# A fused attention and expert kernel on one core: the scatter of an expert's rows is moved behind its test, the gathers into the front half of the tile

## The chip, the cores and the metric

The kernel runs on one core of a Trainium2 chip, as one program. The metric is the device time in microseconds of one execution; the median of the runs shown is 710.27 us.

## The reference, cut to what matters

Attention and a first dense layer make `x`, 1536 rows of 512. The change lies in the last layer, a mixture of eight experts: a row that is not skipped goes through the one expert that its gate picks, and every other row is copied.

```python
def _moe2_ref(x, w_skip, w_gate, w1, w2):
    do_compute = x @ w_skip > 0
    out = x.copy()
    xc = x[do_compute]
    logits = xc @ w_gate
    e_idx = np.argmax(logits, axis=1)
    ...
    for e in range(E):
        mask = e_idx == e
        h = np.maximum(xc[mask] @ w1[e], 0.0)
        y[mask] = gate_w[mask, None] * (h @ w2[e])
    out[do_compute] = xc + y
    return out
```

Per expert `w1` is 512 x 1024 and `w2` 1024 x 512, both float32.

## The kernel before

The first stages (attention, then the first dense layer) fill the time up to about 480 us and are not touched. The second dense layer writes `x` twice, to the scratch tensor `x2d` and to the output, and the routing writes a list `LT`: for each expert up to twelve blocks of 128 rows, each with a row to fetch, a row to write and the gate's weight. Unused places name a row out of bounds, which the scatter leaves out.

`moe2` then goes through the experts. Each expert has one **tile** of 128 rows that always runs, and up to eleven **further tiles** (`extras`), nested in branches on the number of rows that the routing counted, a value that only the run knows. In this run expert 0 has five further tiles, expert 7 has one, the six between have none.

All matmuls are done on values split in two: a high part that ScalarE writes (`w2h`, `xh`, `th`) and the rest that is left, which VectorE or GpSimd subtracts (`w2l`, `xl`, `tl`). A tile is: 12 matmuls for the first half of the hidden layer and the relu, 12 for the second half with the transposes of the first half in between (`hidden`), 24 matmuls into `y`, and `finish`, where VectorE scales `y`, adds it to the fetched rows and leaves the result in the same buffer. In the middle of the second part `prepare(e + 1)` transposes and splits the rows of the next expert.

The order on each engine is the order in which the code is written; nothing reorders it. Four things run beside the matmuls of tile e:

- **Weights.** The sixteen half chunks of expert e + 1 are split (`Moe2Weights.split`, lines 371 to 379), dealt out over the tile by `aside`. ScalarE writes each high part; the rest is VectorE's for twelve of them and GpSimd's for numbers 3, 7, 11 and 15 (`POOLK`). Raw weights arrive in a ring of nine buffers of 512 KB; after each odd half chunk its buffer is free and `load` issues the next load from SyncE's queue, in order, so a load behind one that waits also waits. High and low parts have two sets, used by experts in turn, so expert e + 1's set is free to be written only when expert e - 1 and its further tiles are done.
- **Gathers.** `gather(e + 2)` fetches the rows of the expert after next with an indirect DMA from GpSimd's queue, into one of three buffers `XF`. It takes the buffer that expert e - 1 used, so it needs that expert's scatter to have landed.
- **The pull.** `enlist(e)` and `pull(0)` on GpSimd copy the list of the expert's further blocks and fetch the first of them into `XE`, before it is known whether a further tile runs.
- **Scatter.** At the end of `finish` an indirect DMA on GpSimd's queue writes the tile's rows to the output. The two scatters of an expert with a further tile both write the output and are kept in order.

The test for a further tile (line 619) is taken by each engine for itself. On its untaken side an engine adds to its semaphores what the branch would have added. GpSimd also does so for the semaphores of its DMAs (`INC_SWDGE_SEM` in the trace), and it first waits until the DMAs before the branch have landed. `hint` tells TensorE's queue early which way the branch goes.

Of the kernel before, what the change touches and what calls it, by code (L numbers as in the profile page):

```python
# [22 lines left out]
NT = B * S  # L23
DM = H * D
F1 = 768
E2 = 8
# [485 lines left out]
def fetch(nc, xg, x2d, m):  # L512
    nc.gpsimd.indirect_dma_start(out=xg, out_offset=None, in_=x2d,  # L513
                                 in_offset=bass.IndirectOffsetOnAxis(ap=m[:, 0:1], axis=0))


def moe2(tc, nc, m2, ident, rt, XF, x2d, out):
    pool = tc.alloc_tile_pool(name="m2", bufs=1, side="left", reuse_waits="tile")
    LT, extra = rt["LT"], rt["plan"]
    XH = [[pool.tile([P, NC1, P], F32R, name=f"x{x}{i}") for x in "hl"] for i in range(3)]  # L520
    m2.open(pool, RING[1])
    XE = [pool.tile([P, DM], F32, name=f"xe{i}") for i in range(3)]
    PL = [pool.tile([P, CMAX, 4], I32, name=f"pl{i}") for i in range(2)]
    PM = [pool.tile([P, 4], I32, name=f"pm{i}") for i in range(3)]
    nc.gpsimd.memset(PL[0], 0)
    with tc.tile_pool(name="ps3", bufs=1, space=PSUM, reuse_waits="tile") as ps:

        tiles = [{"e": e, "xg": XF[e % 3], "m": LT[:, e * CMAX], "x": XH[e % 2]} for e in range(E2)]

        def gather(e):  # L530
            if e < E2:
                fetch(nc, tiles[e]["xg"], x2d, tiles[e]["m"])

        def enlist(e):
            nc.gpsimd.tensor_copy(out=PL[0][:, 0:CMAX - 1], in_=LT[:, e * CMAX + 1:(e + 1) * CMAX])  # L535

        def pull(i):
            nc.gpsimd.tensor_copy(out=PM[i % 3], in_=PL[0][:, 0])  # L538
            fetch(nc, XE[i % 3], x2d, PM[i % 3])
            nc.gpsimd.tensor_copy(out=PL[1], in_=PL[0])  # L540
            nc.gpsimd.tensor_copy(out=PL[0][:, 0:CMAX - 1], in_=PL[1][:, 1:CMAX])  # L541

        def turn(src):
            tp = ps.tile([P, 4, P], F32, tag="tp", name="tp", bufs=3)
            for c in range(4):
                nc.tensor.transpose(tp[:, c], src[:, c * P:(c + 1) * P], ident)
            return tp

        def halves(src, h, l):
            nc.scalar.activation(out=h, in_=src, func=AF.Copy)  # L550
            nc.vector.tensor_tensor(out=l, in0=src, in1=h.bitcast(F32), op=ALU.subtract)  # L551

        def prepare(e):
            if e < E2:
                halves(turn(tiles[e]["xg"]), *tiles[e]["x"])

        def ready(i):
            halves(turn(XE[i]), *XH[2])

        def hidden(d, n):  # L560
            d["hT", n] = h, l = [pool.tile([P, 4, P], F32R, tag="t" + x, name="t" + x, bufs=2) for x in "hl"]
            halves(turn(d["r", n]), h, l)

        def mm1(d, n, cr):
            if ("h", n) not in d:
                d["h", n] = ps.tile([P, 512], F32, tag="h", name="h", bufs=3)
            h, l = d["x"]
            for c in cr:
                for i, (a, lo) in enumerate(((h, 0), (h, 1), (l, 0))):
                    nc.tensor.matmul(d["h", n], lhsT=a[:, c], rhs=m2.w1(d["e"], c, n, lo),  # L570
                                     start=(c == 0 and i == 0), stop=(c == NC1 - 1 and i == 2))

        def relu(d, n):
            d["r", n] = pool.tile([P, 512], F32, tag="r", name="r", bufs=2)
            nc.scalar.activation(out=d["r", n], in_=d["h", n], func=AF.Relu)

        def mm2(d, fr):
            if fr[0] == 0:
                d["y"] = ps.tile([P, DM], F32, tag="y", name="y", bufs=2)
            for f in fr:  # L580
                h, l = d["hT", f // 4]
                for i, (a, lo) in enumerate(((h, 0), (h, 1), (l, 0))):
                    nc.tensor.matmul(d["y"], lhsT=a[:, f % 4], rhs=m2.w2(d["e"], f, lo),  # L583
                                     start=(f == 0 and i == 0), stop=(f == NF2 - 1 and i == 2))

        def finish(d):
            ot = d["xg"]
            nc.vector.scalar_tensor_tensor(out=ot, in0=d["y"], scalar=d["m"][:, 2:3].bitcast(F32),
                                           in1=ot, op0=ALU.mult, op1=ALU.add)
            nc.gpsimd.indirect_dma_start(  # L590
                out=out, out_offset=bass.IndirectOffsetOnAxis(ap=d["m"][:, 1:2], axis=0),
                in_=ot, in_offset=None, bounds_check=NT - 1, oob_is_err=False)

        def tile(d, aside=lambda n: None, ahead=lambda: None, then=lambda: None):
            aside(0)
            mm1(d, 0, (0, 1, 2, 3))
            relu(d, 0)
            aside(1)
            mm1(d, 1, (0, 1))
            hidden(d, 0)  # L600
            mm1(d, 1, (2, 3))
            relu(d, 1)
            ahead()
            aside(2)
            mm2(d, (0, 1))
            hidden(d, 1)
            aside(3)
            mm2(d, (2, 3))
            then()
            aside(4)  # L610
            mm2(d, (4, 5, 6, 7))
            finish(d)

        def hint(e, i):
            tc.mark_branch_hint_location(f"x{e}_{i}", extra[e] > i, engines=[mybir.EngineType.PE])

        def extras(d, i=0):
            last = i + 1 == CMAX - 1
            with tc.If(extra[d["e"]] > i, label=f"x{d['e']}_{i}"):  # L619
                def more():  # L620
                    return tc.If(extra[d["e"]] > i + 1)

                def then():
                    with more():
                        ready((i + 1) % 3)

                if i == 0:
                    ready(0)
                if not last:
                    with more():  # L630
                        pull(i + 1)
                tile({"e": d["e"], "xg": XE[i % 3], "m": PM[i % 3], "x": XH[2]},
                     ahead=lambda: last or hint(d["e"], i + 1), then=(lambda: None) if last else then)
                if not last:
                    extras(d, i + 1)

        prepare(0)
        gather(1)
        for e in range(E2):
            todo = list(range(16)) if e + 1 < E2 else []  # L640

            def aside(n):
                k = DEAL[e > 0][n]
                for j in todo[:k]:
                    m2.split(e + 1, j)
                    m2.load(1)
                del todo[:k]

            m2.load(sum(RING) if e == 0 else 0)

            def ahead():
                enlist(e)
                pull(0)
                hint(e, 0)

            def then():
                prepare(e + 1)
                gather(e + 2)

            tile(tiles[e], aside, ahead, then)  # L660
            extras(tiles[e])
    pool.release()


# [455 lines left out]
```

## Time and profile before

| what | us |
|---|---|
| median of the runs shown (3) | 710.27 (709.78 to 713.14) |
| the profiled execution | 706.31 |
| its span, first to last instruction | 704.4 |
| TensorE busy in the span | 649.9 (92%) |
| VectorE busy | 421.7 (60%) |
| ScalarE busy | 336.3 (48%) |
| GpSimd busy | 311.4 (44%) |
| DMA, mean rate | 124 GB/s |

The profiled execution takes 1.9 us more than its span and lies 0.56% below the median. Shares of busy time are means over stages with different limits, so they say little on the last stage, which is the last third of the span; there windows by tile are read. A row of the view by time has start, duration, engine, line, operation, output and inputs, and in brackets how long the engine was idle before it and what ended that. A name such as `POOLq L619` is an instruction of the engine's queue itself (a branch, a wait), which counts as idle time of the engine.

### The profile page before, as it was taken

The page shows a single profiled execution, that of the slowest core. Times are in us where ns is not written, and L with a number is a line of the kernel's source. Part 1 is how long each engine was busy: PE and PEld are TensorE (multiplying, and loading weights), DVE is VectorE, ACT ScalarE, POOL GpSimd, SP SyncE. Part 2 cuts the span into 40 slices and gives each one's busy share as a digit, 9 for nine tenths or more (in the row PEclk, how much of TensorE's full clock was granted, in tenths as well). Part 3 has the DMA queues.
Part 4 walks back from the last instruction along what each step waited for, and adds up shares of the span by engine and source line. Part 5 has one row for each costly group of instructions (what it writes and reads, how often), then busy time and mean ns, then how long its engine had stood idle before and what let it go on. Part 6 is the DMA issues. An engine that isn't in the chain of part 4 may idle for free. (4 is left out here: it accounts for less than half of the span.)

```text
span 704.4 us, 9584 instructions
## 1 busy us (share of the span) xinstructions
PE 649.9 (92%) x3361; PEld 476.7 (68%) x3361; DVE 421.7 (60%) x652; ACT 336.3 (48%) x648; POOL 311.4 (44%) x246
## 2 busy tenths in 40 slices
PE   6798999999999998999999999999799988897884
PEld 2444555555555546999999997886588766675663
DVE  4698868878685483656656652753522276676511
ACT  6665666766665661323223222554322266676510
POOL 1495767767676861322122200343413065555620
PEclk9799999999999999999999999999999999999997
DMA  7454214213003003024304131679701057777510
GB/s 254 168 157 157 90 45 157 69 46 112 23 1 116 0 1 151 19 102 150 117 32 150 44 137 60 209 265 309 275 31 54 23 182 253 257 245 270 182 35 12
DMA packets 31472, 87.40 MB, mean 124 GB/s; under 512 B 4066, under 2 KB 4450, under 8 KB 30608
## 3 DMA queue, kind: packets, MB, share of 16 engines
q1 hardware_dynamic: 28144, 78.21, 32.0%
q0 software_dynamic: 3232, 8.07, 3.6%
q8 instruction: 40, 0.66, 0.4%
q14 instruction: 56, 0.46, 0.2%
HBM read 77.35 MB, written 10.18 MB: 124 GB/s over the span
## 5 line engine op out<-in xcount | busy, mean ns | idle before, releaser
L832 POOL TENSOR_TENSOR sum<-sum,Pt 128x768 f32<-128x768 f32 x60 | 117.1, 1955 | 32.0 <-ACT Pt L827 31.9
L827 ACT ACTIVATE Pt<-psb 128x384 f32<-128x384 f32 x192 | 83.7, 488 | 63.0 <-PE psb L825 62.2
L792 DVE TENSOR_REDUCE negm<-psa 128x1 f32<-128x768 f32 x86 | 82.0, 954 | 42.7 <-PE psa L790 42.4
L217 PE MATMUL m<-xh,whi 128*128 128x384 f32 x288 | 97.7, 339 | 2.9 <-DVEq L923 2.8
L217 PE MATMUL m<-xl,whi 128*128 128x384 f32 x288 | 96.6, 335 | 0.0
L217 PE MATMUL m<-xh,wlo 128*128 128x384 f32 x288 | 96.6, 335 | 0.0
L377 DVE TENSOR_TENSOR w2l<-ring,w2h 128x512 fp32r<-128x512 f32 x100 | 75.7, 808 | 33.3 <-ACT w2h L375 21.5
L839 PE MATMUL pso<-Pt,V 128*64 128x384 f32 x384 | 82.5, 511 | 0.0
L375 ACT ACTIVATE w2h<-ring 128x512 fp32r<-128x512 f32 x128 | 71.7, 623 | 20.9 <-PEq L619 11.3
L823 PE MATMUL psb<-S 128*128 128x384 f32 x192 | 75.8, 395 | 0.3 <-ACT S L767 0.3
L823 PEld LDWEIGHTS psb<-S 128*128 128x128 f32 x192 | 36.4, 190 | 53.3 <-ACT Pt L827 23.1
L825 PE MATMUL psb<-S 128*128 128x384 f32 x192 | 65.4, 340 | 0.0
L217 PEld LDWEIGHTS m<-xh,whi 128*128 128x128 f32 x288 | 54.1, 188 | 6.0 <-DVEq L923 3.5
L377 POOL TENSOR_TENSOR w2l<-ring,w2h 128x512 fp32r<-128x512 f32 x28 | 38.8, 1393 | 40.6 <-DMA ring<-in_dram 20.5
L217 PEld LDWEIGHTS m<-xh,wlo 128*128 128x128 f32 x288 | 54.1, 188 | 0.0
L217 PEld LDWEIGHTS m<-xl,whi 128*128 128x128 f32 x288 | 54.1, 188 | 0.0
L334 POOL TENSOR_TENSOR wlo<-wide,whi 128x512 fp32r<-128x512 f32 x18 | 23.4, 1300 | 69.4 <-ACT whi L333 53.7
L570 PE MATMUL h<-w2h,xh 128*128 128x512 f32 x112 | 48.1, 429 | 6.0 <-ACTq L619 2.7
L551 DVE TENSOR_TENSOR tl<-tp,th 128x512 fp32r<-128x512 f32 x28 | 19.3, 689 | 55.8 <-ACT th L550 50.3
L583 PE MATMUL y<-w2h,th 128*128 128x512 f32 x112 | 48.1, 430 | 3.3 <-ACT th L550 2.8
L583 PE MATMUL y<-w2h,tl 128*128 128x512 f32 x112 | 45.6, 407 | 4.4 <-DVE tl L551 4.3
L570 PE MATMUL h<-w2h,xl 128*128 128x512 f32 x112 | 46.1, 412 | 1.9 <-DVE xl L551 1.9
(185 smaller groups left out, 1219.4 us busy)
## 6 DMA issues: line engine op xcount, KB each, us to landing
ring<-in_dram SPq DMA_DIRECT2D x64, 512.0 KB
R<-in_dram SPq DMA_DIRECT2D x32, 384.0 KB
wraw<-in_dram SPq DMA_DIRECT2D x6, 1536.0 KB
Z<-in_dram SPq DMA_DIRECT2D x16, 384.0 KB
V<-in_dram SPq DMA_DIRECT2D x8, 384.0 KB
oraw<-in_dram SPq DMA_DIRECT2D x6, 512.0 KB
traw<-in_dram SPq DMA_DIRECT2D x6, 512.0 KB
x2d<-x SPq DMA_DIRECT2D x12, 256.0 KB
```

What stands on the lines that cost most here:

```text
L217: nc.tensor.matmul(pt, lhsT=l[:, w, c], rhs=r[b][c][:, a:a + BLK], start=(n == 0), stop=(n == 3 * NC1 - 1))
L334: self.nc.gpsimd.tensor_tensor(out=lo, in0=self.x, in1=hi.bitcast(F32), op=ALU.subtract)
L375: self.nc.scalar.activation(out=h, in_=r, func=AF.Copy)
L377: eng.tensor_tensor(out=l, in0=r, in1=h.bitcast(F32), op=ALU.subtract)
L570: nc.tensor.matmul(d["h", n], lhsT=a[:, c], rhs=m2.w1(d["e"], c, n, lo), start=(c == 0 and i == 0), stop=(c == NC1 - 1 and i == 2))
L583: nc.tensor.matmul(d["y"], lhsT=a[:, f % 4], rhs=m2.w2(d["e"], f, lo), start=(f == 0 and i == 0), stop=(f == NF2 - 1 and i == 2))
L792: nc.vector.tensor_reduce(out=d["negm"][:, t, h:h + 1], in_=tl[:, 0:S], axis=AX.X, op=ALU.max, negate=True)
L823: nc.tensor.matmul(tl, lhsT=S1[:, 2 + h, k * P:(k + 1) * P], rhs=S1[:, h, cut(j)], start=True, stop=False, skip_group_check=True)
L825: nc.tensor.matmul(tl, lhsT=S2[:, 2 + h, k * P:(k + 1) * P], rhs=S2[:, h, cut(j)], start=False, stop=True, skip_group_check=True)
L827: nc.scalar.activation(out=pt[:, cut(j)], in_=tl, func=AF.Exp, scale=0.125)
L832: eng.tensor_tensor(out=d["sum", h], in0=d["P", h, 0] if k == 1 else d["sum", h], in1=pt, op=ALU.add)
L839: nc.tensor.matmul(d["o"][64 * h:64 * h + 64, i], lhsT=d["V"][:, k, h], rhs=d["P", h, k][:, i * BLK:(i + 1) * BLK], start=(k == 0), stop=( ...
```

## The change

The scatter is taken out of `finish` and becomes a function of its own. For the tile of expert e it is called after the expert's test and its further tiles: at the head of the round of expert e + 1, and for the last expert at the program's end. A further tile's scatter stays where it was. Enlist and pull move from the middle of the tile to its head, behind that scatter; for expert 0 ahead of the whole loop. The gather for expert e + 2 moves from the last third of the tile to a point behind the first group of matmuls (`mid`).

```diff
@@ finish, tile
             nc.vector.scalar_tensor_tensor(out=ot, in0=d["y"], scalar=d["m"][:, 2:3].bitcast(F32),
                                            in1=ot, op0=ALU.mult, op1=ALU.add)
+
+        def scatter(d):
             nc.gpsimd.indirect_dma_start(
                 out=out, out_offset=bass.IndirectOffsetOnAxis(ap=d["m"][:, 1:2], axis=0),
-                in_=ot, in_offset=None, bounds_check=NT - 1, oob_is_err=False)
-
-        def tile(d, aside=lambda n: None, ahead=lambda: None, then=lambda: None):
+                in_=d["xg"], in_offset=None, bounds_check=NT - 1, oob_is_err=False)
+
+        def tile(d, aside=lambda n: None, mid=lambda: None, ahead=lambda: None, then=lambda: None):
             aside(0)
             mm1(d, 0, (0, 1, 2, 3))
             relu(d, 0)
             aside(1)
+            mid()
             mm1(d, 1, (0, 1))
@@ extras
-                tile({"e": d["e"], "xg": XE[i % 3], "m": PM[i % 3], "x": XH[2]},
-                     ahead=lambda: last or hint(d["e"], i + 1), then=(lambda: None) if last else then)
+                x = {"e": d["e"], "xg": XE[i % 3], "m": PM[i % 3], "x": XH[2]}
+                tile(x, ahead=lambda: last or hint(d["e"], i + 1), then=(lambda: None) if last else then)
+                scatter(x)
@@ the loop over experts
         prepare(0)
+        enlist(0)
+        pull(0)
         gather(1)
         for e in range(E2):
...
-            def ahead():
+            if e:
+                scatter(tiles[e - 1])
                 enlist(e)
                 pull(0)
-                hint(e, 0)
-
-            def then():
-                prepare(e + 1)
-                gather(e + 2)
-
-            tile(tiles[e], aside, ahead, then)
+            tile(tiles[e], aside, lambda: gather(e + 2), lambda: hint(e, 0), lambda: prepare(e + 1))
             extras(tiles[e])
+        scatter(tiles[E2 - 1])
```

GpSimd is the one engine on which rows change places. Its order for the round of expert 1 before, from behind expert 0's further tiles to the test (`w2l` are splits, `pl` and `pm` the list and its first block, `xe` the pulled rows, `xf` the gathered ones):

```order
L377 TENSOR_TENSOR w2l01_4194<-ring03_4183,w2h01_4186 128x512
L377 TENSOR_TENSOR w2l03_4196<-ring00_4180,w2h03_4188 128x512
L535 COPY pl0_4812<-LT_4459 128x44
L538 COPY pm0_4814<-pl0_4812 128x4
L513 DMA xe0_4809<-x2d_74,pm0_4814 128x512
L540 COPY pl1_4813<-pl0_4812 128x48
L541 COPY pl0_4812<-pl1_4813 128x44
L377 TENSOR_TENSOR w2l05_4198<-ring02_4182,w2h05_4190 128x512
L513 DMA xf0_4201<-x2d_74,LT_4459 128x512
L377 TENSOR_TENSOR w2l07_4200<-ring11_4790,w2h07_4192 128x512
L590 DMA out_0_dram<-xf1_4202,LT_4459 1536x512
L619 COMPARE_AND_BRANCH
```

The same round after the change:

```order
L592 DMA out_0_dram<-xf0_4201,LT_4459 1536x512
L535 COPY pl0_4812<-LT_4459 128x44
L538 COPY pm0_4814<-pl0_4812 128x4
L513 DMA xe0_4809<-x2d_74,pm0_4814 128x512
L540 COPY pl1_4813<-pl0_4812 128x48
L541 COPY pl0_4812<-pl1_4813 128x44
L377 TENSOR_TENSOR w2l01_4194<-ring03_4183,w2h01_4186 128x512
L377 TENSOR_TENSOR w2l03_4196<-ring00_4180,w2h03_4188 128x512
L513 DMA xf0_4201<-x2d_74,LT_4459 128x512
L377 TENSOR_TENSOR w2l05_4198<-ring02_4182,w2h05_4190 128x512
L377 TENSOR_TENSOR w2l07_4200<-ring11_4790,w2h07_4192 128x512
L622 COMPARE_AND_BRANCH
```

The scatter ahead of the test was that of this expert (`xf1`); now the round begins with that of the expert before (`xf0`), and the gather that refills `xf0` follows in the same round. The last DMA ahead of the test is now this gather.

The last round, that of expert 7, before:

```order
L535 COPY pl0_4812<-LT_4459 128x44
L538 COPY pm0_4814<-pl0_4812 128x4
L513 DMA xe0_4809<-x2d_74,pm0_4814 128x512
L540 COPY pl1_4813<-pl0_4812 128x48
L541 COPY pl0_4812<-pl1_4813 128x44
L590 DMA out_0_dram<-xf1_4202,LT_4459 1536x512
L619 COMPARE_AND_BRANCH
```

And the end of GpSimd's program after the change, behind the nested further tiles of expert 7 (an `ISA` row is the untaken side of a test, with its waits; 1118 is the end of the program):

```order
L622 ISA
L622 UNCONDITIONAL_BRANCH
L592 DMA out_0_dram<-xf1_4202,LT_4459 1536x512
L1118 UNCONDITIONAL_BRANCH
L1118 ISA
```

Expert 7's own scatter (`xf1`), once ahead of the test for its further tiles, is now the program's last work.

## Rows read from the trace of the kernel before

**Rows 1.** Windows by tile, tiles 1 to 6: stretch, us, busy by engine, clock, DMA.
```profile
566.05:582.93 16.88, 13.21 (x61) 9.95 (x61) 12.08 (x17) 10.88 (x21) 12.18 (x12) 1.00 0.64 219
582.93:598.02 15.09, 14.91 (x60) 11.05 (x61) 10.30 (x16) 11.11 (x22) 8.00 (x9) 0.89 0.69 242
598.02:614.81 16.79, 14.78 (x61) 11.09 (x61) 11.28 (x17) 11.31 (x22) 8.97 (x11) 0.90 0.75 257
614.81:628.40 13.59, 13.29 (x60) 9.88 (x61) 11.97 (x17) 11.09 (x22) 5.30 (x6) 1.00 0.83 275
628.40:647.68 19.28, 14.76 (x61) 11.02 (x61) 11.79 (x17) 11.76 (x22) 11.78 (x13) 0.91 0.74 251
647.68:664.38 16.70, 13.43 (x61) 9.88 (x61) 12.33 (x17) 11.52 (x21) 10.19 (x11) 1.00 0.70 239
```

**Rows 2.** SyncE's waits, tiles 1 to 6: us in total, times, longest.
```profile
SPq L365 <- POOL w2l L377: 38.9, 9, 9.1
SPq L368 <- POOL w2l L377: 18.3, 8, 3.8
```

**Rows 3.** GpSimd by time, one round: start, us, instruction, idle before it.
```profile
628.33 2.54 POOL L377 TENSOR_TENSOR w2l<-ring,w2h 128x512 fp32r<-128x512 f32 x2 [7.96 <-PE y L583]
630.83 0.21 POOL L535 COPY pl<-LT 128x44 int32<-128x44 int32 x1
...
633.53 0.21 POOL L541 COPY pl<-pl 128x44 int32<-128x44 int32 x1
...
635.57 1.27 POOL L513 DMA_INDIRECT xf<-x2d,LT  x1
...
638.32 1.28 POOL L590 DMA_INDIRECT out_dram<-xf,LT  x1 [0.17 <-issue]
646.36 2.54 POOL L377 TENSOR_TENSOR w2l<-ring,w2h 128x512 fp32r<-128x512 f32 x2 [6.77 <-DMA ring<-in_dram]
```

**Rows 4.** The same view, first round, and around the last round's start.
```profile
571.00 3.44 POOL L377 TENSOR_TENSOR w2l<-ring,w2h 128x512 fp32r<-128x512 f32 x2 [3.28 <-PE tp L546]
...
656.20 1.27 POOL L590 DMA_INDIRECT out_dram<-xf,LT  x1 [0.17 <-issue]
663.26 2.52 POOL L377 TENSOR_TENSOR w2l<-ring,w2h 128x512 fp32r<-128x512 f32 x2 [5.79 <-DMA out_dram<-xf,LT]
```

**Rows 5.** Line 619 on GpSimd's queue: ns min/median/max.
```profile
L619 POOLq INC_SWDGE_SEM  x1: 1022/1022/1022, 662.1 to 662.1; - x1
```

**Rows 6.** TensorE by time, four places; then the window of the last further tile.
```profile
582.93 0.50 PE L570 MATMUL h<-w2h,xh 128*128 128x512 f32 x1 [2.71 <-ACTq L619]
...
636.27 0.50 PE L583 MATMUL y<-w2h,th 128*128 128x512 f32 x1 [1.71 <-ACT th L550]
...
642.70 1.12 PE L546 MATMUL tp<-cs,xf 128*128 128x128 f32 x4 [2.43 <-DMA xf<-x2d,LT]
...
679.07 0.66 PE L546 MATMUL tp<-cs,xe 128*128 128x128 f32 x4 [2.49 <-DMA xe<-x2d,pm]
...
676.60:694.40 17.80, 0.00 (x0) 0.00 (x0) 0.90 0.10 32
```

**Rows 7.** VectorE by time; then tile 4's window, line 377 alone: VectorE, GpSimd.
```profile
570.32 2.98 DVE L377 TENSOR_TENSOR w2l<-ring,w2h 128x512 fp32r<-128x512 f32 x3 [1.58 <-ACT w2h L375]
...
602.45 0.69 DVE L377 TENSOR_TENSOR w2l<-ring,w2h 128x512 fp32r<-128x512 f32 x1 [3.79 <-DVEq L619]
...
631.47 0.69 DVE L377 TENSOR_TENSOR w2l<-ring,w2h 128x512 fp32r<-128x512 f32 x1 [2.43 <-DVEq L619]
...
614.81:628.40 13.59, 9.42 (x12) 2.68 (x3) 1.00 0.83 275
```

**Rows 8.** Chain of waits, two pieces (start, us); then the program's end, ns.
```profile
677.97 2.77 DMA out_dram<-xf,LT
...
695.48 0.98 POOL out_dram L590
...
L1116 POOLq DRAIN  x3: 46/106/3991, 699.6 to 704.1; - x3
```

## Prediction

> **What bounds the kernel now.** I read the time by tile first, then who holds SyncE, then GpSimd's own order of time, then TensorE's pauses. Tile e is the first tile of expert e; the further tiles of expert 0 end at 566.05, where tile 1 starts. The windows by tile [rows 1] show what to look at: tile 4 takes 13.59 us, tiles 5 and 6 take 19.28 and 16.70 for the same matmuls, and in tile 5 the granted clock is 0.91. So the last tiles hold time that is not TensorE's work. The SyncE waits say who keeps the weights back [rows 2]: the ring loads wait 38.9 + 18.3 = 57 us for the GpSimd splits on line 377, because a ring buffer is free only after its second half is split, and that is a GpSimd split for every second buffer.
>
> GpSimd's round [rows 3] shows why those splits come late. The two early splits of a round run at 628.33, the enlisting and pulling from 630.83 to 633.74, the gather for the tile after next at 635.57, the scatter at 638.32. Then nothing runs until 646.36, 6.77 us. This is the untaken test: its other side waits until every GpSimd DMA has landed, and only then adds to their semaphores. In the round after, the scatter is issued at 656.20 and the next split starts at 663.26, idle 5.79 for the scatter [rows 4], of which the adding takes 1.02 [rows 5]. A round is 646.36 - 628.33 = 18.0 us; from 571.00 to 663.26 lie five, 18.5 each [rows 3, 4]. TensorE needs less: tile 1 took 16.88 - 2.71 = 14.2 of work with all its data there [rows 1, 6]. So GpSimd falls behind tile by tile: its first split of tile 1 starts 5 us after the tile, that of tile 6 (started 647.68) 15.6 us after. TensorE pays late [rows 6]: 1.71 us at 636.27 (ScalarE stands behind a split whose load is late), 2.43 at 642.70 (the gather issued at 635.57 has only just landed, 7.1 us on), 2.49 at 679.07 (expert 7's pulled rows).
>
> **The change part by part.** No instruction is added or taken away; on GpSimd they change places, and TensorE, ScalarE and VectorE keep their order.
>
> The test. It now comes after the last split, and the scatter after it, at the head of the next round. The test's wait no longer holds a DMA issued just ahead of it, but it still waits for the gather of this round, which is now the last one issued. So the round becomes: scatter 1.28, enlist and pull 2.9, two splits 2.54 [rows 3], together 6.7, with gaps 7.0. Then the gather. It refills the buffer that this round's scatter empties, so it waits for the scatter to land: at most 663.26 - 656.20 - 1.02 = 6.0 us after its issue, and 646.36 - 638.32 - 1.0 = 7.0 in the round before [rows 3 to 5]. That is hidden behind the 7.0 of other work, just so. The gather lands 7.1 later if it meets ring traffic as at 635.57, and 2.8 later if it lands as the lone scatter at 677.97 did [rows 8]; the two remaining splits (1.3 each) run meanwhile. With 1.0 for the adding the round is 7.0 + 7.1 + 1.0 = 15.1 us, or 7.0 + 1.3 + 2.6 + 1.0 = 11.9 if landings are quick. I take 15.1, since the rows with ring traffic are those of this stage. Against 18.5, GpSimd gains 3.4 a round.
>
> What that gives. At first it gives nothing: after expert 0 the first round starts with the scatter, enlist and pull, 4.2 us ahead of the split that stood there at 571.00, so the first loads go out later. The ring is full then, and tile 2 doesn't need them before it starts. With rounds of 15.1 from 571.0 the fourth starts at 616.3 and its first split at 620.5, against 628.33; the fifth splits at 635.6, against 646.36. The loads of tile 5 and 6 come 8 to 11 us earlier and the waits at 636.27 and 642.70 go, with the low clock behind the second.
>
> What is late next in those tiles is VectorE. After an untaken test it starts late, with nothing to wait for that the trace shows: 3.79 us in tile 3, 2.43 in tile 5 [rows 7]. Tile 3 took 16.79 with that, 2.6 over 14.2. For tile 5 I take 2.43 / 3.79 of it, 1.7: 15.9. Tile 6 gets 14.2. Together 30.1 against 35.98: **5.9 saved**. Tile 4 holds 2.68 us of GpSimd splits now, two of them [rows 7]; with all four it goes from 13.59 to 14.2: **0.6 lost**. The three tiles take 49.57 now; their bounds are 3 x 13.6 = 40.8 (saved 8.8) and tile 3's time for two of them (13.6 + 33.6 = 47.2, saved 2.4).
>
> Expert 7's further tile. Its pull stands behind the scatter of tile 6 and is issued some 2.5 us into tile 7, over 6 us ahead of its use with nothing else in flight. Of the 2.49 about 0.5 stays for the branch. The granted clock of its 17.80 us is 0.90 [rows 6], 1.8 of it missing, part of that while TensorE stood anyway; of the clock I take 1.2 back. **3.2 saved**; 0 if VectorE or the branch is late there, as a lower bound.
>
> The end. Expert 7's own scatter, hidden in its further tile until now, is issued last, behind the further tile's scatter, and both write the output, so it waits for that to land and for the test. Its price is at least its issue, 1.28 [rows 3], and at most issue and landing: the scatter at 677.97 took 2.77 from issue to landing, so with what lies between two issues 4 [rows 8]. The drain of 3.99 us at the end starts at 699.6, 4.1 after the last scatter's issue at 695.48, when by the 2.77 it has landed; so the drain isn't waiting for that, and it should cover the new landing: I take the lower end, **1.3 lost**.
>
> The front. The pull of expert 0 now stands ahead of the gather for tile 1, both some 1 us from their old place, and both wait for the same writes. The further tiles' first transposes come sooner, but VectorE is busy there until its own finish; I give it nothing, with 1 us either way.
>
> The Trainium skill, page "SBUF — State Buffer", section "SBUF: two separate sides", speaks against putting GpSimd's splits beside VectorE's: an instruction that holds the port pair these two share blocks the other for its full length. By that rule the tiles would not get shorter; this is the second rival below.
>
> **Sum.** -5.9 + 0.6 - 3.2 + 1.3 = -7.2 us on the profiled execution's 706.31 (span 704.4): 699.1, or 0.9898 of it. The median of the runs shown is 710.27, 0.56% above that execution; times 0.9898 it is **703.0**. With all its terms at their good ends (-8.8 - 3.2 + 1.3 - 1) the forecast is -11.7, 698.5; with the tiles at -2.4 and the end at +4 it is -1.6, 708.7. About 0.5%, or 3.5 us, is what a measurement of this kernel can tell from no change.
>
> **The rivals.**
> 1. *ScalarE at the tile's end (slower).* Between tiles 1 and 2 TensorE stood 2.71 us for ScalarE, which came late out of the untaken test [rows 6], and tile 2 then ran at a granted clock of 0.89, 1.7 us of its 15.09 [rows 1]. In tiles 4 to 6 ScalarE now waits for loads and TensorE waits with it, so its test lies under other waits. If on-time loads put it as close to TensorE's end as in tile 1, each of the three ends costs 4.4: -7.2 + 13.2 = +6.0, 716.3. It decides at the third end: with two it is +1.6, no change. Against it: between tiles 3 and 4, loads in flight too, nothing of it is seen. 0.12.
> 2. *VectorE as the bound (no change).* Three of its splits took 2.98 us beside GpSimd's, where one alone takes 0.69 [rows 7]. If each GpSimd split costs VectorE its whole 1.27, a tile on VectorE is 12 x 0.69 + 4 x 1.27 + 2.8 (four other instructions of 0.7) = 16.2, and tiles 1 to 6 are 97 against the 98.3 from 566.05 to 664.38. Left is the further tile less the end, -1.9: 708.4. Against it: three such splits began inside tile 1's 14.2 of work and the fourth right behind it. 0.13. The rule of the Trainium skill above is this rival; the 14.2 doesn't bear it out.
> 3. *The test still waits as long.* If the gather, held by the scatter, lands so late that a round stays at 18, nothing but the end moves: -1.9, 708.4. It needs landings of 10 us where 7.1 is the longest read. 0.08.
> 4. *More.* Tiles 2 and 3 lose their pauses as well, 15.09 + 16.79 - 2 x 14.2 = 3.5 more with the good ends, -15, 695. 0.05; nothing in the trace ties those pauses to GpSimd.
>
> **How the numbers follow.** The forecast has 0.62. The predicted time is 703.0. The range takes in the forecast and the unchanged cases, 697.5 to 710, and leaves out rivals 1 and 4 and a few per cent of the rest. Faster, under 706.7: 0.56 of the forecast, rival 4, and a little of rivals 2 and 3, 0.63. Same: the rest of the forecast and of rivals 2 and 3, 0.25. Slower: rival 1, 0.12.
>
> **What would show it.** On GpSimd: no idle stretch of 6 us ahead of the first split, rounds near 15 us, the scatter followed at once by enlist and pull. SyncE's waits for GpSimd under 40 us. TensorE without the pauses for the gather and for the pulled rows; tiles 5 and 6 under 33 us together. At the end two scatters, and the span's end 1 to 3 us further behind the last matmul. I am wrong if rounds stay at 18, or if they shrink and the tiles don't.

## The result and the profile after

The changed kernel takes 703.7 us (median of 6 runs, 699.83 to 705.42), the kernel before 711.7 beside it (6 runs): a ratio of 0.9895, with a 95% interval of 0.9858 to 0.9932. Measured once more, beside 29 runs of before (707.14 to 719.37), it is 703.42 and 0.9854 (0.9799 to 0.9909). So the gain is 1.0 to 1.5%, 7 to 10 us, and the predicted 703.0 met it. How the gain arises is another matter.

The profiled execution of after took 703.54 us, its span is 701.6. TensorE's tiles now start at 565.28, 578.75, 592.80, 611.76, 627.30, 643.77 and 660.79 (tiles 1 to 7). The windows by tile 1 to 6, in the columns of [rows 1]:

```profile
565.28:578.75 13.47, 13.20 (x60) 9.98 (x61) 10.79 (x15) 10.79 (x22) 7.95 (x10) 1.00 0.39 131
578.75:592.80 14.05, 13.46 (x60) 9.88 (x61) 12.48 (x19) 11.21 (x22) 7.02 (x10) 1.00 0.85 295
592.80:611.76 18.96, 15.88 (x60) 11.90 (x61) 12.71 (x17) 11.63 (x22) 11.83 (x13) 0.82 0.81 271
611.76:627.30 15.54, 13.22 (x61) 9.93 (x61) 13.59 (x17) 11.41 (x21) 8.79 (x11) 1.00 0.88 308
627.30:643.77 16.47, 13.74 (x61) 9.89 (x61) 12.12 (x16) 11.53 (x21) 8.15 (x11) 1.00 0.84 283
643.77:660.79 17.02, 14.56 (x60) 10.93 (x61) 12.45 (x17) 11.43 (x21) 10.61 (x13) 0.90 0.65 235
```

Against [rows 1] tiles 1 to 6 take 95.5 us instead of 98.3. The gain stands in tile 1 (13.47 for 16.88), and in tile 5 (16.47 for 19.28); tiles 3 and 4 became longer. Of tile 1's 3.4 us, 2.7 are TensorE's pause for ScalarE's test [rows 6], which is gone there. Tile 1's DMA share fell from 0.64 to 0.39, since its loads now start later; the last section returns to how the two hang together.

GpSimd by time, one round, as in [rows 3]:

```profile
621.81 1.02 POOL L592 DMA_INDIRECT out_dram<-xf,LT  x1 [6.17 <-DVE w2l L377]
622.82 0.76 POOL L535 COPY pl<-LT 128x44 int32<-128x44 int32 x1
...
626.08 2.52 POOL L377 TENSOR_TENSOR w2l<-ring,w2h 128x512 fp32r<-128x512 f32 x2
628.74 0.99 POOL L513 DMA_INDIRECT xf<-x2d,LT  x1
629.75 2.54 POOL L377 TENSOR_TENSOR w2l<-ring,w2h 128x512 fp32r<-128x512 f32 x2
640.05 1.01 POOL L592 DMA_INDIRECT out_dram<-xf,LT  x1 [7.76 <-DVE w2l L377]
```

The idle stretch of some 6 us is still there (5.8 to 7.8), now ahead of the scatter. The round is 640.05 - 621.81 = 18.2 us; over the five from 570.96 to 656.64 it is 17.1, against 18.5 before and 15.1 predicted. The SyncE waits of tiles 1 to 6 did not fall either: 49.1 + 8.6 = 57.7 us for GpSimd, 57 in [rows 2].

```profile
SPq L365 <- POOL w2l L377: 49.1, 6, 11.1
SPq L368 <- POOL w2l L377: 8.6, 8, 1.5
```

What did change is what TensorE waits for. The view of waits for TensorE, tiles 1 to 6 (us in total, times, longest), of before:

```profile
PE y L583 <- DVE tl L551: 4.3, 4, 1.8
PE tp L546 <- DMA xf<-x2d,LT: 3.0, 2, 2.4
PE y L583 <- ACT th L550: 2.8, 2, 1.7
PE h L570 <- ACTq L619: 2.7, 1, 2.7
```

and of after:

```profile
PE y L583 <- ACT th L550: 6.3, 3, 2.9
PE y L583 <- DVE tl L551: 2.2, 3, 1.0
PE h L570 <- ACTq L622: 1.6, 2, 1.2
```

Gathered rows are not waited for any more (3.0 before), VectorE's `tl` half as long, ScalarE's test (`ACTq`) 1.6 us instead of 2.7; ScalarE's `th` is waited for longer. Behind tile 7, the first tile of expert 7, the pause for the pulled rows, 2.49 us in [rows 6], is 0.69:

```profile
673.69 0.66 PE L546 MATMUL tp<-cs,xe 128*128 128x128 f32 x4 [0.69 <-DMA xe<-x2d,pm]
```

The program's end, from the last matmul to the end of the span, is 12.1 us instead of 10.0.

### The profile page after: what moved, and what is told of

The parts are those of the page before. It is cut to its first block, busy times and chain, and to the rows that moved or that the text cites. A ratio compares the mean times of both kernels' runs of the same rounds, so it can differ in the third digit from the quotient of the medians.

```text
span 701.6 us, 9589 instructions
## 1 busy us (share of the span) xinstructions
PE 648.2 (92%) x3361; PEld 475.5 (68%) x3361; DVE 426.4 (61%) x652; ACT 336.5 (48%) x648; POOL 306.9 (44%) x246
## 5 line engine op out<-in xcount | busy, mean ns | idle before, releaser
L377 DVE TENSOR_TENSOR w2l<-ring,w2h 128x512 fp32r<-128x512 f32 x100 | 78.8, 837 | 28.6 <-ACT w2h L375 22.0
L551 DVE TENSOR_TENSOR tl<-tp,th 128x512 fp32r<-128x512 f32 x28 | 19.3, 689 | 55.4 <-ACT th L550 49.9
L792 PE MATMUL psa<-S 128*128 128x512 f32 (+1 forms) x172 | 47.2, 356 | 4.0 <-DVE negm L794 2.1
```

The lines of the kernel that those rows point to most:

```text
L377: eng.tensor_tensor(out=l, in0=r, in1=h.bitcast(F32), op=ALU.subtract)
L792: nc.tensor.matmul(tl[:, a:e], lhsT=S1[:, h, t * P:(t + 1) * P], rhs=S1[:, 2 + h, a:e], start=True, stop=True, skip_group_check=True)
```

## The experiments

Each time below is a median in us; the ratio is to the kernel before on the same chip, with its 95% interval. Single executions of one kernel lie 0.7 to 2.6% apart, and their time goes with TensorE's mean granted clock, though not strictly (before: 715.8 us of span at 0.960, 705.4 at 0.978). A single profile is one sample, and times are compared by medians. Three of the profiles below are the fastest of their kernel's runs (`after_again`, `before_again`, `xf4_splits_first`), that of `nopoolk` is the slowest. The theory on trial is the prediction's: the scatter ahead of the test costs GpSimd its round, and late splits cost TensorE its time. Its first rival is that the earlier gathers and pulls bring the gain; other rivals came up as the results came in.

**The scatter alone, the rest alone, and both kernels again.** `s_only` moves only the scatter behind the test:

```diff
-        enlist(0)
-        pull(0)
...
             if e:
                 scatter(tiles[e - 1])
-                enlist(e)
-                pull(0)
-            tile(tiles[e], aside, lambda: gather(e + 2), lambda: hint(e, 0), lambda: prepare(e + 1))
+            def ahead():
+                enlist(e)
+                pull(0)
+                hint(e, 0)
+            def then():
+                prepare(e + 1)
+                gather(e + 2)
+            tile(tiles[e], aside, ahead=ahead, then=then)
```

> Only the scatter moves behind the test (the last expert's to the end); enlisting, pulling and gathering keep their old places. Theory A (the scatter ahead of the test is what cost GpSimd its round): most of the gain is here, ratio to before about 0.990, 704 to 705 us, rounds on GpSimd 17 us or less. Theory B (the gain is the earlier gathers and pulls, whose rows TensorE waited for): no gain, since the gather issued late in the round is now what the test waits for; rounds 18 to 18.5 us, idle 6 to 8 us at the test, the pauses for gathered rows stay or grow, and the end costs 2 us: ratio 1.000 to 1.005, 711 to 715 us.

Measured: 711.73, ratio 0.9990 (0.9959 to 1.0022). No gain, as theory B has it. Rounds are 17.9 us and idle 6.2 to 7.5 at the test.

`gh_only` is the changed kernel with the scatter back ahead of the test:

```diff
-                scatter(tiles[e - 1])
                 enlist(e)
                 pull(0)
...
+            scatter(tiles[e])
             extras(tiles[e])
-        scatter(tiles[E2 - 1])
```

> The scatter stands ahead of the test again; the gather stays in the front half and enlist and pull at the head. Theory A: the gain is gone, ratio 0.998 to 1.002, rounds 18 to 18.5 us with 6 us idle for the scatter. Theory B: the gain stays and the 2 us at the end come back, ratio 0.985 to 0.988, 701 to 703 us, with no pause of TensorE for gathered or pulled rows although the rounds on GpSimd are no shorter.

Measured: 707.23, ratio 0.9955 (0.9918 to 0.9993), between the theories. Rounds are 18.0 with 6.9 to 7.6 us idle for the scatter, and no gathered row is waited for in tiles 1 to 6. The view of TensorE's waits shows what takes their place, ScalarE's `th`, whose splits wait for loads:

```profile
PE y L583 <- ACT th L550: 7.4, 5, 2.2
PE y L583 <- DVE tl L551: 3.0, 2, 1.5
```

So neither half gives the 7 to 10 us; the two together do. Whether the halves add up stays open: by the ratios they gain 0.1% and 0.45%, and the whole 1.05% and 1.46%; by the plain medians beside the same runs of before they gain 1.6 and 6.1 us, and the whole 9.9.

> The changed kernel once more, to have a second profile of it and its time beside the same runs of before: ratio 0.986 to 0.993. A second profile tells which of the differences between the first two profiles repeat: if the +2.2 and +1.9 us of tiles 3 and 4 and the -3.4 us of tile 1 are the change's own, they come again within 0.5 us; if they are where the execution happened to wait, they move to other tiles.

Measured: 703.42, ratio 0.9854 (0.9799 to 0.9909). Its profiled execution is the fastest of its runs (692.94). Tile 1 is 13.49 again, with the same clock (1.00) and nearly the same DMA share (0.42), but tiles 3 to 6 move: 16.75, 17.09, 13.53 and 14.66. So tile 1 belongs to the change; the lengths of tiles 3 to 6 don't repeat. The clock is 1.00 in all six tiles here, where it was 0.82 and 0.90 in tiles 3 and 6 of the first profile. Rounds are 16.0.

> The kernel before once more, for a second profile: ratio 1.000 within 0.004. If the pauses of 2.71 us after tile 1, 2.43 us in tile 5 and 2.49 us ahead of the last further tile are its own, they come again; the stages ahead of tile 0 should agree with 483 us within 2 us.

Measured: 714.22, ratio 1.0028 (0.9996 to 1.0059). The pause behind tile 1 comes again, longer (3.9 us for ScalarE's test), and so does the one for the pulled rows (2.2); the one for gathered rows in tile 5 doesn't, and TensorE waits 8.7 us for `tl`.

**The front and the end.** `pull0_back` puts expert 0's enlist and pull back into its tile:

```diff
         prepare(0)
-        enlist(0)
-        pull(0)
...
-            tile(tiles[e], aside, lambda: gather(e + 2), lambda: hint(e, 0), lambda: prepare(e + 1))
+            tile(tiles[e], aside, lambda: gather(e + 2), (lambda: (enlist(e), pull(0), hint(e, 0))) if e == 0 else (lambda: hint(e, 0)), lambda: prepare(e + 1))
```

> The changed kernel with one thing undone: expert 0's enlist and pull stand in the middle of its tile again, not ahead of the loop. If that place alone gives the 3.2 us of tile 0 with its further tiles (33.0 to 33.7 us from the first matmul of tile 0 to the second further tile with the old place, 29.9 with the new), this stretch takes 33 us again, with a pause of about 1.5 us for the pulled rows and a clock of 0.90, and the time is 3 us over that of the changed kernel, 705 to 708. If the gather's place gives it, the stretch stays at 30.

Measured: 705.03, ratio 0.9896 (0.9848 to 0.9944), 1.3 to 1.6 us over the two medians of the changed kernel, which is not clear of noise. The profile shows the 33.2 us and a clock of 0.90, with a pause of 3.03 for the pulled rows. `pull0_only` is that part alone, in the kernel before:

```diff
         prepare(0)
+        enlist(0)
+        pull(0)
         gather(1)
...
-                enlist(e)
-                pull(0)
+                if e:
+                    enlist(e)
+                    pull(0)
```

> The kernel before with one part of the change alone: expert 0's enlist and pull ahead of the loop. If the earlier pulled rows give the 3 us of tile 0 and its further tiles, no pause for pulled rows is left in the further tiles' start, the stretch from tile 0 to tile 1 falls from 83 to 80 us, and the time is 2 to 3 us under that of before, ratio 0.995 to 0.997. If it is the gather's place, nothing changes.

Measured: 711.12, ratio 1.0010 (0.9971 to 1.0050). In the profile the stretch is shorter, but no gain can be measured. The windows of the stretch from tile 0 to the second further tile, of before and of `pull0_only`:

```profile
483.18:515.92 32.74, 28.45 (x125) 21.70 (x125) 16.53 (x21) 14.56 (x27) 12.75 (x16) 0.95 0.70 245
```

```profile
486.43:515.89 29.46, 26.91 (x124) 20.51 (x125) 13.82 (x21) 14.67 (x27) 12.69 (x14) 1.00 0.77 279
```

About 1.6 us of the 3.3 lie in the clock (0.95 of it granted in 32.74 us, all of it in 29.46), and that part doesn't come each time: in five of the ten profiles with this order of the front (`last_back`, `nopoolk`, `xf4`, `xf4_hints` and `xf4_splits_first`) the stretch takes 31.2 to 34.3 us at a clock of 0.90 to 0.95, with a pause for VectorE's `xl` of 1.6 to 2.7. In four of the other five that pause is 1.3 to 1.7 and the clock stays at 1.00. By the profiles the front gives 0 to 3 us; by the medians of these two experiments 0 to 1.6, neither clear of noise.

`last_back` puts expert 7's scatter back ahead of its test:

```diff
+            if e + 1 == E2:
+                scatter(tiles[e])
             extras(tiles[e])
-        scatter(tiles[E2 - 1])
```

> The changed kernel with expert 7's own scatter back ahead of its test. If the second scatter at the end costs 2.1 us (12.1 to 12.3 us from the last matmul to the span's end against 10.0), the end takes 10.0 again and the time is 2 us under that of the changed kernel, 700 to 702. If the drain hides it after all, nothing changes.

Measured: 700.36, ratio 0.9846 (0.9801 to 0.9891), and 10.2 us from the last matmul to the end. By the profiles the end costs 2 us; the time fits that.

**GpSimd's wait.** `xf4` is `last_back` with a fourth gather buffer, in the space of constants that are no longer read, so that the gather can stand first in the round (the lines that lay out the buffer are left out here):

```diff
-        tiles = [{"e": e, "xg": XF[e % 3], ...
+        tiles = [{"e": e, "xg": XF[e % 4], ...
...
+            gather(e + 2)
             if e:
                 scatter(tiles[e - 1])
                 enlist(e)
                 pull(0)
-            tile(tiles[e], aside, lambda: gather(e + 2), lambda: hint(e, 0), lambda: prepare(e + 1))
+            tile(tiles[e], aside, lambda: None, lambda: hint(e, 0), lambda: prepare(e + 1))
```

> As last_back, and a fourth buffer for gathered rows (in space of constants that are no longer read), so that the gather no longer has to wait for the scatter of the same round: it is issued first in the round and has landed when the test comes. Theory A (the wait of GpSimd's test keeps GpSimd behind, and that keeps the loads back): the 6 us of idle ahead of the scatter go to 2 or less, rounds fall from 16 to 17 us to the tile's own 13.5 to 14, SyncE's waits for GpSimd fall by half or more, tiles 3 to 6 come near 14 each, and the time is 5 to 9 us under last_back, 692 to 697. Theory B (the loads themselves bound tiles 3 to 6, at a DMA share of 0.9): rounds still follow the tiles at 15 to 16, the DMA share stays 0.8 to 0.9, and the time is within 3 us of last_back. Theory C (VectorE, slowed by GpSimd's splits beside its own): the tiles stay, and TensorE's pauses are for VectorE.

Measured: 697.75, ratio 0.9799 (0.9756 to 0.9843). What theory A has of the wait comes for the most part: rounds fall to 14.9, GpSimd's idle time ahead of the gather to 2.0 to 4.4 us, tiles 1 to 6 to 89.2, and `th` is waited for 0.7 us. What it has of the time doesn't: that is 2.6 us under `last_back`, within the 3 us of theory B and with overlapping intervals, and TensorE's largest wait is now VectorE's `xl`, as in theory C. SyncE's waits for GpSimd fall only from 57.7 to 47.5, so they are a poor witness: the ring is emptied in order, and some engine is always its last. The view of TensorE's waits:

```profile
PE h L571 <- DVE xl L552: 4.2, 3, 2.1
PE h L571 <- ACTq L623: 1.9, 4, 0.7
PE y L584 <- DVE tl L552: 1.0, 2, 0.8
PE y L584 <- ACT th L551: 0.7, 1, 0.7
```

The DMA engines are nearly full in some tiles (share 0.95 in tile 2 and 0.97 in tile 4).

**The place of GpSimd's splits.** `nopoolk` is the changed kernel with `POOLK = ()`:

> The changed kernel with all sixteen splits of an expert on VectorE, none on GpSimd, so no load waits for GpSimd. Theory A: SyncE's waits for GpSimd are gone, VectorE takes 16 x 0.69 + 2.8 = 13.8 us a tile, tiles 1 to 6 take 14 each or 84 together (95.5 and 90.6 in the two profiles of the changed kernel), and the time is 693 to 698. Theory B (loads): tiles 3 and 4 stay at 16 or more, time 700 or more. Theory C (VectorE is the bound as soon as it has all the splits): TensorE waits for VectorE's parts (xl, tl) in every tile, tiles of 15 and more, time 703 to 710.

Measured: 703.88, ratio 0.9862 (0.9815 to 0.9909): the same as the changed kernel. The time lies in the ranges of theories B and C, but not for their reasons: tile 3 takes 13.80 us at a DMA share of 0.92, and `tl` isn't the largest wait. VectorE takes all splits and TensorE waits only 3.8 us for `tl`, but the loads of tile 1 go out early again (DMA share 0.80), and ScalarE's test is late three times, as the waits of TensorE show:

```profile
PE h L570 <- ACTq L622: 7.3, 3, 2.9
PE y L583 <- DVE tl L551: 3.8, 6, 2.0
```

`xf4_splits_first` is `xf4` with enlist and pull behind GpSimd's first two splits, as they stood before the change:

```diff
-                enlist(e)
-                pull(0)
-            tile(tiles[e], aside, lambda: None, lambda: hint(e, 0), lambda: prepare(e + 1))
+            tile(tiles[e], aside, (lambda: (enlist(e), pull(0))) if e else (lambda: None), lambda: hint(e, 0), lambda: prepare(e + 1))
```

> The kernel with four gather buffers, with enlist and pull moved behind GpSimd's first two splits, so that the first loads of tile 1 are issued 2 to 4 us earlier. Theory E (the late loads of tile 1, DMA share 0.36 to 0.42 there, are what tiles 2 to 5 lack): the share in tile 1 rises, tiles 2 to 5 get 2 to 3 us shorter in all, time 695 or less. Theory D (loads in flight draw out the fetch behind ScalarE's test at the end of tile 1): ScalarE's stretch there grows from 3.0 to 4 or more and TensorE pauses 1 to 3 us between tiles 1 and 2, so that the gain is given back: 697 to 700.

Measured: 711.09, ratio 0.9998 (0.9953 to 1.0042). This one move gives back all that `xf4` had gained, 13 us by the medians, more than either theory has; rounds are 15.9, shorter than in `gh_only`. Both theories' signs come: the DMA share of tile 1 rises to 0.63 from 0.36, and ScalarE's stretch at tile 1's test to 5.7 us from 3.2, but TensorE waits only 0.8 us for it. The profile, the fastest of twelve runs, has 95.1 us in tiles 1 to 6 where `xf4` has 89.2, so it shows about half of the 13. TensorE's waits:

```profile
PE y L584 <- DVE tl L552: 12.1, 8, 2.4
PE h L571 <- ACTq L623: 0.8, 1, 0.8
```

Nearly all of them, 12.1 of 13.7 us, are for VectorE's `tl`. One of these, in VectorE's, GpSimd's and TensorE's rows by time:

```profile
621.47 1.89 DVE L378 TENSOR_TENSOR w2l<-ring,w2h 128x512 fp32r<-128x512 f32 x3 [1.09 <-ACT w2h L376]
...
625.08 4.83 DVE L378 TENSOR_TENSOR w2l<-ring,w2h 128x512 fp32r<-128x512 f32 x3 [0.87 <-ACT w2h L376]
629.84 0.68 DVE L552 TENSOR_TENSOR tl<-tp,th 128x512 fp32r<-128x512 f32 x1
...
625.57 2.56 POOL L378 TENSOR_TENSOR w2l<-ring,w2h 128x512 fp32r<-128x512 f32 x2
628.05 0.70 POOL L536 COPY pl<-LT 128x44 int32<-128x44 int32 x1
...
630.57 0.50 PE L584 MATMUL y<-w2h,tl 128*128 128x512 f32 x1 [2.36 <-DVE tl L552]
```

Three splits of VectorE take 1.89 us alone, and 4.83 while GpSimd's two splits and its copy run, 2.9 more for 3.3 of GpSimd's work beside them. The first of the three alone takes 3.61 us, up to the end of that copy; the other two take 0.7 each. What stands behind them is the second `tl`, and TensorE waits 2.36 us for it. In `xf4` GpSimd's splits run together at the tile's end. There they stretch VectorE as much (three splits took 5.22 us at 622.07), but the next result that TensorE needs of VectorE is the next tile's `xl`, and for that it waits 4.2 us in all six tiles.

**What is left.** `xf4_hints` is `xf4` with the hint on the test's way given to all four engines (`engines=ENGINES` for `engines=[mybir.EngineType.PE]`):

> The kernel with four gather buffers, in which the hint on which way the test goes, given in the middle of the tile, is given to ScalarE, VectorE and GpSimd too, not to TensorE alone. Theory D (what is left at the test is the fetch of the code on its other side, which ring traffic draws out: 2.5 to 3.4 us on ScalarE in tiles 1, 4 and 5, 5 to 6 on VectorE in tiles 2 and 4, 4.6 to 6.2 on GpSimd, from the compare to the first instruction of the untaken side): with the hint these fall to 1 us or so, the idle time of GpSimd ahead of the gather falls from 2 to 4 us to about 1.5, tiles 2 and 4 lose their 2 us pauses for VectorE, and the time is 3 to 6 us under that of the kernel with four buffers alone, 692 to 695. Rival: the engines' wait there is for something else (work of their own, semaphores), or the hint does nothing for them: time within 2 us of 697.8, the same stretches as long.

Measured: 701.49, ratio 0.9835 (0.9777 to 0.9893). No gain: TensorE waited 7.1 us for ScalarE's test, up to 3.56 at once. Theory D's remedy falls; whether the hint did anything on these engines stays open.

`xf4_late_splits` is `xf4` with `POOLK = (9, 11, 13, 15)`:

> The kernel with four gather buffers, in which GpSimd takes half chunks 9, 11, 13 and 15 of an expert instead of 3, 7, 11 and 15: as many, all in the last third of the tile, and the first ring buffers of a round are freed by VectorE. Theory F (GpSimd's splits stretch VectorE's beside them, and cost time where VectorE's next result is one that TensorE waits for, the tl of the second group of matmuls): the splits stay behind that place, TensorE's waits for tl stay at 1 to 2 us over tiles 1 to 6 (12.1 with the splits first), and since no early load waits for GpSimd, the time is 692 to 698. Theory D (early loads draw out the fetch of the untaken side): as in the kernel without splits on GpSimd, ScalarE comes late out of the test of tile 1, TensorE waits 5 us or more for ScalarE's tests over tiles 1 to 6, and the time is 699 to 704. If tl is waited for 8 us or more with the splits at the end, theory F is wrong, time 705 or more.

Measured: 697.43, ratio 0.9791 (0.9729 to 0.9853), the time of `xf4`. `tl` is waited for 5.5 us, more than the 1 to 2 expected and less than the 8 that would speak against theory F. In the middle the DMA engines are nearly full, by the windows of tiles 2 to 4 (last columns: clock, DMA share, GB/s); that they bound the tiles is not shown, since TensorE's waits are still for `tl`:

```profile
584.68:598.90 14.22, 13.23 (x61) 10.00 (x61) 12.90 (x15) 11.23 (x22) 11.19 (x13) 1.00 0.96 340
598.90:614.13 15.23, 13.45 (x60) 9.87 (x61) 12.11 (x18) 11.19 (x22) 11.65 (x12) 1.00 0.95 329
614.13:628.84 14.71, 13.03 (x61) 10.01 (x61) 12.45 (x17) 11.18 (x21) 11.04 (x12) 1.00 0.96 343
```

`xf4` and `xf4_late_splits` are faster than both kernels of the case, each measured beside before on its own chip: 14 us less than before, and some 6 less than after.

## Why the prediction was right, and where it was not

The time was right, but not by the way that the prediction gave, and that much is luck: its largest term, 5.3 us for tiles 4 to 6, stands on a step that failed. Nor does the first pair of profiles hold the 8 us of the medians. Their spans differ by 2.8 us: tiles 1 to 6 by -2.8, the front by -2.8, expert 7's two tiles by -1.2, the end by +2.1, and the part ahead of tile 0 by +1.9, which differs by 3.6 between the two profiles of after alone. Without that part the first pair gives -4.7 and the mean of two pairs -11.5, where the prediction had -7.2.

The kernels side by side (rounds in us, means of four or five; TensorE's waits and tiles 1 to 6 from the one profile of each):

| kernel | ratio | GpSimd round | TensorE for VectorE (`tl`, `xl`) | for `th` | tiles 1 to 6 |
|---|---|---|---|---|---|
| before | 1 | 18.5 | 4.3 | 2.8 | 98.3 |
| before, again | 1.003 | 19.3 | 10.2 | 0 | 103.2 |
| `pull0_only` | 1.001 | 18.9 | 9.5 | 0 | 100.4 |
| `s_only` | 0.999 | 17.9 | 9.9 | 1.3 | 96.7 |
| `gh_only` | 0.996 | 18.0 | 3.0 | 7.4 | 98.9 |
| after | 0.990 | 17.1 | 2.6 | 6.3 | 95.5 |
| after, again | 0.985 | 16.0 | 1.7 | 3.5 | 90.6 |
| `pull0_back` | 0.990 | 16.7 | 1.7 | 5.7 | 93.8 |
| `last_back` | 0.985 | 17.0 | 4.1 | 5.9 | 96.0 |
| `nopoolk` | 0.986 | 15.3 | 3.8 | 0 | 98.9 |
| `xf4_hints` | 0.984 | 15.4 | 1.7 | 1.9 | 93.7 |
| `xf4` | 0.980 | 14.9 | 5.2 | 0.7 | 89.2 |
| `xf4_late_splits` | 0.979 | 14.6 | 5.5 | 0 | 88.8 |
| `xf4_splits_first` | 1.000 | 15.9 | 12.1 | 0 | 95.1 |

Two things act in this table. Where GpSimd's splits come behind enlist and pull, late in the tile, TensorE waits 1.7 to 5.5 us for VectorE; where two of them come first, 9.5 to 12.1 (4.3 in the first profile of before, which was a fast one of its kind). With that given, the waits for `th`, that is for late loads, go with GpSimd's round: 7.4 at 18.0, 3.5 to 6.3 from 16.0 to 17.1, 1.9 at 15.4, 0.7 at 14.9, 0 at 14.6. That would be why neither half brings the whole: the scatter alone shortens what isn't waited for, the rest alone leaves the round at 18. A third wait, ScalarE's test, is not in the table; it holds back `nopoolk` and `xf4_hints`, 7.3 and 7.1 us. That the place of the splits decides is shown by the pair `xf4` and `xf4_splits_first`, for the kernel with four buffers; that it does so from before to after rests on the table; that the shorter round is the cause of the smaller waits for `th` rests on this order of the kernels and on rows like these of ScalarE in after, where the load is what its split waits for, and `th` stands behind it:

```profile
597.96 1.15 ACT L375 ACTIVATE w2h<-ring 128x512 fp32r<-128x512 f32 x2 [1.49 <-DMA ring<-in_dram]
600.22 1.15 ACT L375 ACTIVATE w2h<-ring 128x512 fp32r<-128x512 f32 x2 [1.10 <-DMA ring<-in_dram]
601.27 0.58 ACT L550 ACTIVATE th<-tp 128x512 fp32r<-128x512 f32 x1
```

Point by point:

- *The test* (round 15.1): the direction held, the size didn't. From the gather's issue to the next scatter's the sum had 7.1 + 1.0 = 8.1 us; the rows show 10.2 as the mean of five (11.3 in the round above). The median landing of a gather in tiles 1 to 6 is 7.9, and the step left out what follows the adding and the other side's start. The round fell by 1.4 to 2.5 instead of 3.4 us. Rival 3 (it stays at 18) came nearer to the first profile than the forecast.
- *What that gives* (loads of tiles 5 and 6 come 8 to 11 us earlier; 5.9 saved): this step failed. The first splits of the fourth and fifth round start at 626.08 and 643.86 in after, 2.3 and 2.5 us earlier than before. With enlist, pull and scatter ahead of it the first split starts 9.7 to 16.9 us after the tile in after, where before it was 5 to 18. So the loads, counted from the start of a tile, are mostly later, and "at first it gives nothing" was wrong: the most certain gain is tile 1, 13.47 and 13.49 for 16.88 and 20.56. Tiles 1 to 6 gave 2.8 us in the first pair of profiles and 7.7 on the mean of two each, by causes that the step didn't have.
- *VectorE as what is late next*, and rival 2: the prediction asked how many splits a tile holds and set the sharing aside, since tile 1 took 14.2. What counts is where they stand. The price of rival 2, a GpSimd split costing VectorE nearly its whole length, is borne out by the 2.9 us above; it was paid in the kernel before already, and the change moves most of it out of the way. The rule of the Trainium skill named there (page "SBUF — State Buffer", section "SBUF: two separate sides") agrees with that row; the prediction used it against the change, and it speaks for it.
- *Rival 1*, ScalarE at the tile's end: it is real, and it turned round as well. It costs 2.7 and 3.9 us in before, 7.3 in `nopoolk`, 1.6 and 1.5 in after, where none of it stands behind tile 1, whose loads start late there.
- *Expert 7's further tile* (3.2 saved): tile 7 and the further tile fell from 29.98 and 31.16 us in the two profiles to 28.75 and 26.72: 1.2 in the first pair, 2.8 on the mean. Right within what the profiles tell; the pause for the pulled rows gave 1.8 of the 2.0 expected.
- *The end* (1.3 lost): 2.1, inside the bounds. The drain does cover the landing, as the prediction said. But the second scatter is issued 5.2 us behind the first, whose landing and the test it waits for:

```profile
690.67 1.02 POOL L592 DMA_INDIRECT out_dram<-xe,pm  x1 [18.77 <-DVE xe L588]
695.84 0.99 POOL L592 DMA_INDIRECT out_dram<-xf,LT  x1 [4.15 <-issue]
```

- *The front* (nothing, 1 us either way): some 3 us in five of ten profiles of this order, so by them the bound was too narrow; by the medians 0 to 1.6, so what it gives stays open.
- *What would show it*: the pauses for gathered and pulled rows went, the two scatters and the 1 to 3 us at the end came, and tiles 5 and 6 took 33.5 us where under 33 was named. The idle stretch, the round and SyncE's waits, which were to show the main step, showed it wrong.

What stays open: how much of the gain each cause has. The profiles' waits don't sum up to the times, for one because a wait of TensorE is often followed by a stretch at the lower of its two clock levels (1.2 of 2.4 GHz), as in tile 3 of after (clock 0.82, behind the pause of 2.93 us at 601.90), and not always.

## What to carry to other kernels

Where the work of one engine slows another's beside it, ask which result of the other stands right behind the place that the work moves to: here, with the same splits ahead of a result that TensorE needs, it waited 12.1 us for VectorE, and 5.2 with them behind it, and the kernels lie 13 us apart. A test that waits for DMAs waits for the last one issued, whichever that is; moving one of two only hands the wait to the other, and it goes when the last one gets a buffer of its own and is issued first. And a time that comes out as predicted proves no step: the three witnesses of the main step (the idle stretch, the round, SyncE's waits) had failed here.

## What the runs showed of the hardware that was not expected

How long ScalarE takes out of the untaken test behind tile 1 goes with the DMA traffic in that time. ScalarE's next instruction behind tile 1's test, by time, in before and in after:

```profile
583.00 1.15 ACT L375 ACTIVATE w2h<-ring 128x512 fp32r<-128x512 f32 x2 [4.15 <-ACTq L619]
```

```profile
578.73 1.68 ACT L375 ACTIVATE w2h<-ring 128x512 fp32r<-128x512 f32 x3 [1.41 <-PEq L622]
```

From ScalarE's compare to its first work on the other side the stretch is 577.48 to 583.00 in before and 575.85 to 578.73 in after. The DMA queues in those two windows (packets, MB, share of 16 engines):

```profile
q1 hardware_dynamic: 711, 1.37, 72.0%
q0 software_dynamic: 92, 0.31, 14.5%
q14 instruction: 3, 0.02, 1.4%
q8 instruction: 1, 0.02, 1.2%
```

```profile
q1 hardware_dynamic: 100, 0.41, 44.8%
q0 software_dynamic: 39, 0.10, 10.5%
q8 instruction: 1, 0.02, 2.8%
q14 instruction: 1, 0.01, 0.9%
```

Code arrives by DMA there (the instruction rows), beside ring loads that take 72% and 45% of the engines; the stretch is 5.5 us under the one and 2.9 under the other. Its first packet comes 3.0 us behind the compare in before and 0.8 in after. The fourteen profiles agree at this test: with the DMA engines busy for 30 to 78% of the stretch it takes 2.9 to 3.4 us (eight profiles), with 89% and more 4.4 to 6.7 (six). In `nopoolk`, where tile 1's loads are early again, TensorE waits 2.93 us behind that tile. So in tile 1 later loads seem to have made a shorter tile; no run changes the loads alone. The tests behind tiles 2 and 3 don't follow this: at shares of 95% and more the stretch was 1.8 to 2.9 us in six of nine cases. GpSimd's stretch, from its compare to the first instruction on the other side, is 4.6 to 6.2 us in tiles 1 to 5 of `xf4`, where no landing is waited for; its last part is the idle time that is left there. The Trainium skill, page "Runtime: NRT & Kernel Launch", section "Instruction fetch mechanics", says that a taken branch out of the window that is held makes the sequencer fetch by DMA before it goes on. The rows agree with a fetch there, and suggest that it stands behind the kernel's own loads.
